# Two attentions on one core: the second attention's V in 4096 B rows, its quads in pairs, PV on 64x64 tiles, one PSUM pool

## The chip, the cores and the metric

The kernel runs on one core of one Trainium2 chip. The metric is the device time of one execution in microseconds, the median of several. A core has TensorE (PE, matmuls), VectorE (DVE), ScalarE (ACT), GpSimd (POOL) and SyncE (SP, which issues the DMAs here), each with an instruction stream of its own; semaphores order them. The matmuls' results land in PSUM, which has eight banks of 2 KB on each of 128 partitions. Transfers run on 16 DMA engines.

## The reference

Two attention blocks run on their own inputs, and their outputs are put side by side. Both have 16 batches of 32 queries, a model width of 1024, 32 query heads of 128, and a cache of 1024 keys, all in bf16. Block A has 4 key/value heads (each serves 8 query heads); block B has 32.

```python
q = (x @ wq).reshape(B, Sq, H, Dh).transpose(0, 2, 1, 3)
scores = jnp.einsum("bhqd,bhkd->bhqk", q, k_cache) * (Dh ** -0.5)
p = softmax(scores, axis=-1)
o = jnp.einsum("bhqk,bhkd->bhqd", p, v_cache)
out = o.transpose(0, 2, 1, 3).reshape(B, Sq, H * Dh) @ wo
# A: the same, with k and v repeated 8 times over the heads; result: concatenate([a, b], axis=-1)
```

The caches of B are 134 MB each for K and V, those of A an eighth of that. All that is read from memory comes to 338 MB.

## The kernel before, in words

**Quads.** The work is cut into 128 quads of A and 128 of B. A quad has 128 score rows, one for each partition. In A it is one batch and four query heads that share one K and V. In B it is two batches (`t_`) and two heads (`hh`) with 32 queries each, so four K and four V of 256 KB each belong to it. Four B quads make a group (4 batches, 4 heads, 128 tokens): the index `bp` picks the pair of batches, `hp` the pair of heads.

**A quad's chain of steps** is: scores into two PSUM banks (PE); the row maximum (DVE, `st_max`); the exponential with the row sum (ACT, `st_exp`); the transposes of P by 128 columns (PE, `st_ptr`), and their copy to `PT_sb` (`st_pev`); PV (PE, `st_pv`); the reciprocal of the sum and the normalisation (`st_norm`); the transpose of the output (`st_otr`) and its copy to `OTA_sb` or `OTB_sb`. After each group the output projection (`oproj`) adds into `acc` in SBUF. Between the quads lie the query projections of later blocks.

**Scores of B.** K of two heads of a batch is loaded in rows of 16 keys (4096 B to a partition), and DVE transposes it as 32x32 blocks of f32 into `KBt_sb` (`st_ktrB`, L785). The contraction over 128 then runs in four passes of 32x32 tiles on PE (L827): a pass of a quad has eight matmuls on eight of the 16 tiles, two row tiles to each bank. The queries are brought to the same form by `qprepB_tr` and `qprepB_sh` (`Qshuf`, L638).

**PV of B.** V is loaded by `vsrc` (L763) as eight keys of one head to a partition, 2048 B at a time. Two adjacent bf16 probabilities are transposed as one f32 by four 128x128 transposes (L862). PV has four column tiles of 32, one for each batch and head, and eight steps over the keys (L892):

```python
last = e.matmul(bank(vb)[32 * a:32 * a + 32, 0:Dh], ptc_of(vPT, c, 32 * a, 32 * a + 32), VB_sb[:, kvs, a // 2, a % 2, c, :],
                start=(c == 0), stop=(c == NCH - 1), tile_position=(0, 32 * a))
```

**Buffers.** K of B has two sides of two slots of 512 KB (`KB_sb`), with two more sides for the transposed K. V of B has three sides of two (`VB_sb`). The scores have two fixed pairs of banks (`ps_s`); a pool of four banks (`ps_g`) serves all else.

**What sets the order.** The steps are recorded in a `Prog`, and `list_schedule` lays them out in time: it takes prices for every step from `DUR` and for every packet from `PACKET`, keeps a time at which each engine is free, and picks by priority (the length of the chain behind a step, less `STEP_US` for each quad number). Buffers of a pool (`Virt`) get their place then. For steps marked "any" it chooses ACT or DVE. The result is a fixed order for every engine; at run time only semaphores decide. All loads are issued by SP in that order, so a load that waits for its buffer holds back the loads behind it.

Of the kernel before, what the change touches and what calls it, by code (L numbers as in the profile page):

```python
# [16 lines left out]
NVB_SLOTS = 3  # L17
NKB_SLOTS = 2
# [7 lines left out]
PRIO_BONUS = {}  # L26
PE_MODE = {"scoresB": 2, "Qshuf": 2, "PVB": 1}
MODE_SWITCH = 0.05
LOOK = 0.35
STEP_US = 3  # L30
STEP_NEAR = 0
ACT_FIRST = 0.3
# [3 lines left out]
    "scoresB": (0.216, 0.20), "scoresA": (0.216, 0.20), "PT_trA": (0.49, 0.22), "PT_trB": (0.49, 0.22), "PVA": (0.45, 0.22), "PVB": (0.112, 0.22),  # L36
    "OT_tr": (0.056, 0.22), "KTA_tr": (0.45, 0.22), "Qshuf": (0.107, 0.20), "qprojA": (0.432, 0.20), "qprojB": (0.432, 0.20),
    "oprojA": (0.432, 0.20), "oprojB": (0.432, 0.20), "xT_tr": (0.45, 0.22),
    "exp": (1.10, 0.12), "PT_ev@act": (0.466, 0.13), "norm@act": (0.25, 0.13), "OT_ev@act": (0.11, 0.13), "KTA_ev@act": (0.466, 0.13),
# [8 lines left out]
PACKET = {"kb_dma": (4096, 0.159), "wq_dma": (1024, 0.046)}  # L48
PACKET_DEFAULT = (2048, 0.084)
# [5 lines left out]
def dma_time(op):  # L55
    size, us = PACKET.get(op.name, PACKET_DEFAULT)
    return op.dur / size * us / 16


class _Op:  # L60
    __slots__ = ("eng", "emit", "deps", "sig", "dma_key", "dma_val", "clock", "name", "needs_sig", "waits", "dur", "t0", "t1", "tag", "prio", "idx", "alts", "step")
# [28 lines left out]
SLOTS = {"bank": 4, "P": 3, "PT": 3, "stat": 6, "O": 2}  # L90
BANK_RESERVE = {"pj": 2}


def actual(res):
    out = []
    for r in res:
        if not isinstance(r, Virt):
            out.append(r)
        elif r.cls == "bank":
            out.append(("bank", 4 + r.idx))  # L100
        else:
            out.append((r.cls, r.idx))
    return tuple(out)


class Prog:
# [12 lines left out]
    def add(self, eng, emit, reads=(), writes=(), dma_key=None, name="", dur=None, tag=None, prio=0, wtag=None, rtag=None, claims=()):  # L119
# [7 lines left out]
        if dma_key is None:  # L127
            dur = DUR.get(name, (0.2, 0.1))
        self.specs.append((eng, emit, tuple(reads), tuple(writes), dma_key, name, dur, tag, prio))
# [6 lines left out]
        op.step = self.step  # L136
        op.idx = len(self.ops)
        deps = {}
# [22 lines left out]
        if dma_key is not None:  # L161
            op.dma_key = dma_key
            self.dma_count[dma_key] = self.dma_count.get(dma_key, 0) + 1
# [59 lines left out]
    def list_schedule(self, lat=0.05, look=LOOK):  # L223
        ops = self.ops
        n = len(ops)
        users = [[] for _ in range(n)]
        ndeps = [0] * n
        for op in ops:
            ndeps[op.idx] = len(op.deps)
            for d in op.deps:  # L230
                users[d.idx].append(op.idx)

        def odur(op):
            if op.dma_key is not None:
                return DMA_FIRST + dma_time(op) + DMA_LAST
            return op.dur[0] + op.dur[1]
        bl = [0.0] * n
# [28 lines left out]

        def slot_time(i):

            t = 0.0
            for v in acq[i]:  # L270
                idle = [slot_free[v.cls][x] for x in range(SLOTS[v.cls]) if held[v.cls][x] is None]
                keep = sum(k for kind, k in BANK_RESERVE.items() if kind != v.kind and not any(h is not None and h.kind == kind for h in held["bank"])) if v.cls == "bank" else 0
                if len(idle) <= keep:
                    return None
                t = max(t, sorted(idle)[0])
            return t

        def acquire(i, st):
            for v in acq[i]:
                x = min((x for x in range(SLOTS[v.cls]) if held[v.cls][x] is None), key=lambda x: slot_free[v.cls][x])  # L280
                held[v.cls][x] = v
                v.idx = x

        def release(i, t):
            for v in mentions[i]:
                left[v] -= 1
                slot_free[v.cls][v.idx] = max(slot_free[v.cls][v.idx], t)
                if left[v] == 0:
                    held[v.cls][v.idx] = None
# [12 lines left out]
        dma_free = [0.0]  # L302

# [7 lines left out]
        while True:  # L311
            best = None
            bkey = None
            for eng, lst in ready.items():
# [11 lines left out]
                for i in lst:  # L326
                    s_ = slot_time(i) if acq[i] else 0.0
                    if s_ is not None:
                        at[i] = max(ready_t[i], fe, s_) + sw(i)
                if not at:  # L330
# [21 lines left out]
            if beng == "pe":  # L352
                pe_mode[0] = PE_MODE.get(op.name, 0)
            op.t0 = st
# [10 lines left out]
            order.append(best)  # L365
# [759 lines left out]
```

## Time and profile before

| | us |
|---|---|
| median of 3 runs | 903.28 |
| lowest and highest | 902.01, 904.05 |
| the profiled execution, own time | 904.35 |
| its span, first to last instruction | 902.6 |
| busy: PE, DVE, ACT | 836.3, 745.3, 610.8 |

The profile is of one execution. Its own time is 1.75 us above its span, and 1.07 us above the median of the runs. PE's busy time holds matmuls whose ends are modelled and which overlap, so a busy PE is not one at its peak; PEld is the loading of weights, beside it. SPq is the sequencer that issues the DMAs; its waits are for buffers. The granted clock of PE is 0.985 over the span. The page's groups give these durations, as the mean of one instruction: DVE's transpose of K (L785) 1231 ns, the maximum (L837) 1209, the exponential (L850) 1119, the normalisation on ACT (L908) 370.

### The profile page before, as it was taken

To read this page: it belongs to the slowest core of one execution; us is meant where nothing else is said; L and a number is where in the kernel's file an instruction comes from. 1 tells how busy PE (TensorE), PEld (TensorE's weight loads), DVE (VectorE), ACT (ScalarE), POOL (GpSimd) and SP (SyncE) were. 2 spreads that over 40 slices of the span, in tenths; PEclk is the share of its full clock that TensorE was granted. 3 is DMA by queue.
4 is the path that set the end of the run, shared out by engine and by line. 5 is a ranking of instruction groups with operands and counts; after the bars stand their busy time and mean duration, and the time that the engine had idled before them with its cause. 6 is when DMAs were issued, how large, how long until landed. Compare 5 with 4: busy or idle time off the path is not lost.

```text
span 902.6 us, 29455 instructions
## 1 busy us (share of the span) xinstructions
PE 836.3 (93%) x12864; PEld 481.8 (53%) x12864; DVE 745.3 (83%) x1057; ACT 610.8 (68%) x1384; POOL 1.1 (0%) x8
## 2 busy tenths in 40 slices
PE   6999999999899999999999998999998988999886
PEld 4365555555555555555545455555555554555453
DVE  0578897888887999689887899878979788798885
ACT  3477886677666776676776466776867666586763
POOL 0000000000000000000000000000000000000000
PEclk9999999999999999999999999999999999999999
DMA  9999999999999999999999999999999999999994
GB/s 325 383 389 393 386 385 392 390 393 383 392 387 389 393 380 388 380 386 376 387 385 391 394 369 389 388 393 370 388 387 391 392 391 367 344 393 393 393 377 170
DMA packets 153984, 341.67 MB, mean 379 GB/s; under 512 B 12544, under 2 KB 28928, under 8 KB 153856
## 3 DMA queue, kind: packets, MB, share of 16 engines
q1 hardware_dynamic: 153856, 339.79, 100.6%
q8 instruction: 102, 1.67, 0.8%
q14 instruction: 26, 0.21, 0.1%
HBM read 337.64 MB, written 2.10 MB: 376 GB/s over the span
## 4 chain that ended last, share of the span: by engine, by line
PE 48%; DMA 23%; DVE 19%; ACT 8%; SPq 1%; issue 1%; ACTq 0%; DVEq 0%
DMA KB_sb<-in_B_k_cache_dram 21%; PE ps_s L827 10%; PE ps_g L862 9%; DVE stat L837 8%; DVE KBt_sb L785 8%; PE ps_g L680 6%; ACT P_sb L850 5%; PE ps_g L892 4%; PE ps_g L598 4%; PE ps_g L884 4%; PE ps_g L616 3%; PE ps_s L806 3%; PE ps_g L776 2%; ACT PT_sb L526 1%; PE ps_g L914 1%
## 5 line engine op out<-in xcount | busy, mean ns | idle before, releaser
L785 DVE STREAM_TRANSPOSE KBt_sb<-KB_sb 128x1024 f32<-128x1024 f32 x256 | 311.8, 1231 | 42.5 <-DMA KB_sb<-in_B_k_cache_dram 40.4
L837 DVE TENSOR_REDUCE stat<-ps_s 128x1 f32<-128x1024 f32 x256 | 304.7, 1209 | 50.7 <-PE ps_s L827 34.3
L850 ACT ACTIVATE P_sb<-ps_s,stat 128x1024 bf16<-128x1024 f32 x256 | 285.8, 1119 | 51.5 <-DVE stat L837 50.0
L862 PE MATMUL ps_g<-id,P_sb 128*128 128x128 f32 x1024 | 177.0, 300 | 13.0 <-ACT P_sb L850 4.7
L862 PEld LDWEIGHTS ps_g<-id,P_sb 128*128 128x128 f32 x1024 | 150.5, 207 | 54.9 <-issue 11.1
L827 PE MATMUL ps_s<-KBt_sb,QR 32*32 32x512 bf16 x4096 | 157.2, 399 | 19.5 <-ACT P_sb L850 10.9
L526 ACT COPY PT_sb<-ps_g 128x512 f32<-128x512 f32 x234 | 134.9, 591 | 59.5 <-PE ps_g L862 58.3
L908 ACT ACTIVATE O_sb<-ps_g,stat 128x128 bf16<-128x128 f32 x199 | 71.4, 370 | 63.0 <-PE ps_g L892 32.4
L806 PE MATMUL ps_s<-KTA_sb,QT_sb 128*128 128x512 bf16 x256 | 91.5, 388 | 6.0 <-ACT P_sb L850 5.6
L827 PEld LDWEIGHTS ps_s<-KBt_sb,QR 32*32 32x32 bf16 x4096 | 49.3, 90 | 81.1 <-ACT P_sb L850 17.8
L892 PE MATMUL ps_g<-VB_sb,PT_sb 128*32 128x128 bf16 x4096 | 91.1, 224 | 1.4 <-ACT PT_sb L526 0.9
L892 PEld LDWEIGHTS ps_g<-VB_sb,PT_sb 128*32 128x32 bf16 x4096 | 60.2, 97 | 48.7 <-issue 29.2
L884 PE MATMUL ps_g<-VA_sb,PT_sb 128*128 128x128 bf16 x1024 | 78.8, 220 | 1.8 <-ACT PT_sb L526 0.7
L884 PEld LDWEIGHTS ps_g<-VA_sb,PT_sb 128*128 128x128 bf16 x1024 | 61.6, 98 | 28.2 <-issue 8.5
L616 PE MATMUL ps_g<-wq_sb,xT_sb 128*128 128x512 bf16 x256 | 71.4, 386 | 2.9 <-DMA wq_sb<-in_B_wq_dram 2.8
L680 PE MATMUL ps_g<-woB_sb,OTB_sb 128*128 128x512 bf16 x256 | 68.7, 381 | 4.4 <-ACT OTB_sb L526 1.8
L598 PE MATMUL ps_g<-xT_sb,wq_sb 128*128 128x512 bf16 x256 | 72.0, 385 | 0.3
L680 PE MATMUL ps_g<-woA_sb,OTA_sb 128*128 128x512 bf16 x256 | 63.0, 380 | 1.3 <-DVE OTA_sb L526 1.0
L914 PE MATMUL ps_g<-ident,O_sb 128*128 128x128 bf16 x256 | 51.8, 224 | 3.0 <-ACT O_sb L908 2.0
L850 ACT ACTIVATION_READ_ACCUMULATOR P_sb<-ps_s,stat 128x1 f32 x256 | 51.8, 202 | 0.0
L526 ACT COPY OTA_sb<-ps_g 128x64 f32<-128x64 f32 x114 | 24.7, 216 | 36.7 <-PE ps_g L914 36.1
L691 DVE TENSOR_TENSOR acc<-acc,ps_g 128x512 f32<-128x512 f32 x64 | 41.2, 675 | 8.1 <-PE ps_g L680 7.6
(41 smaller groups left out, 537.5 us busy)
## 6 DMA issues: line engine op xcount, KB each, us to landing
VB_sb<-in_B_v_cache_dram SPq DMA_DIRECT2D x256, 512.0 KB, 8.1
KB_sb<-in_B_k_cache_dram SPq DMA_DIRECT2D x256, 512.0 KB, 9.2
KA_sb<-in_A_k_cache_dram SPq DMA_DIRECT2D x64, 256.0 KB, 7.7
VA_sb<-in_A_v_cache_dram SPq DMA_DIRECT2D x64, 256.0 KB, 8.1
wq_sb<-in_B_wq_dram SPq DMA_DIRECT2D x32, 256.0 KB, 8.6
wq_sb<-in_A_wq_dram SPq DMA_DIRECT2D x32, 256.0 KB, 8.8
woB_sb<-in_B_wo_dram SPq DMA_DIRECT2D x32, 256.0 KB, 9.2
woA_sb<-in_A_wo_dram SPq DMA_DIRECT2D x32, 256.0 KB, 9.1
```

Of the source, the lines that this page charges most:

```text
L526: return e.copy(dst, src) if hasattr(e, "activation") else e.tensor_copy(dst, src)
L598: last = e.matmul(bank(v)[:, 0:tn], wq_sb[:, 0, j, hc * Dh:(hc + 1) * Dh], xT_sb[:, 0, j, t0:t0 + tn], start=(j == 0), stop=(j == DJ - 1))
L616: last = e.matmul(bank(v)[:, 0:CW], xT_sb[:, 1, j, G * P:(G + 1) * P], wq_sb[:, 1, j, :], start=(j == 0), stop=(j == DJ - 1))
L680: last = e.matmul(bank(v)[:, 0:OUTW], OT[:, gp, hh, :], wo_[:, hh, oh * OUTW:(oh + 1) * OUTW], start=(hh == 0), stop=(hh == nh - 1))
L785: pr.add("dve", lambda e: e.transpose(KBt_sb[:, sl, t_, :].bitcast(F32), KB_sb[:, rs, :].bitcast(F32)), reads=[("KB", rs)], writes=[("KBt" ...
L806: pr.add("pe", lambda e, u=u: e.matmul(ps_s[:, vS.idx, u, :], qt[:, q.b, q.hh0:q.hh0 + 4, :].rearrange("p a q -> p (a q)"), KTA_sb[:, sl, ...
L827: last = e.matmul(ps_s[32 * cg:32 * cg + 32, vS.idx, g2, :].rearrange("p (s j) -> p s j", s=16), lhsT, rhs, start=(fp == 0), stop=(fp == 3 ...
L837: pr.add("dve", lambda e: e.tensor_reduce(stat[:, vst.idx, 0:1], ps_s[:, vS.idx, :, :], AXIS.XY, ALU.max, negate=True), writes=vS.res + [v ...
L850: return e.activation(dst, src, ACTF.Exp, bias=stat[:, vst.idx, 0:1], scale=1.0, accum_out=stat[:, vst.idx, 1:2])
L862: last = e.transpose(bank(vb)[:, m * P:(m + 1) * P], p32[:, m:Sk // 2:NPK], id32[:])
L884: last = e.matmul(bank(vb)[:, 0:Dh], ptc_of(vPT, c, 0, P), VA_sb[:, kvs, c, :], start=(c == 0), stop=(c == NCH - 1))
L892: last = e.matmul(bank(vb)[32 * a:32 * a + 32, 0:Dh], ptc_of(vPT, c, 32 * a, 32 * a + 32), VB_sb[:, kvs, a // 2, a % 2, c, :], start=(c == ...
```

## The change

Seven things change together.

- **V of B** is loaded like K: 16 keys of one head to a partition, 4096 B each, two heads in the partitions' halves (`st_dmaB`). A load is 512 KB as before.
- **Two quads of B go together** (`pairB_all`): the two that share batches and differ in `hp`. Their scores are recorded as one step of 16 matmuls on all 16 tiles for each pass (`st_scoresBB`); the second quad has its heads in the other half of the score rows. There are 64 pairs.
- **P of B** is transposed in 32 blocks of 64x64 in bf16, two row halves (`e_ptB`), where four f32 transposes were.
- **PV of B** runs on 64x64 tiles: a tile contracts over the 64 partitions of one head and has 256 columns, the V of both batches (`st_pvBB`). Of the result a row uses the columns of its own batch: the normalisation covers 256 columns, two transposes follow (`st_otr`), and `st_oev` copies the blocks that are wanted. The heads change places in OTB, and `oproj` picks the rows of wo to match.
- **PSUM** is one pool of eight banks. Scores take two neighbours, at one of three places.
- **Slots of K, transposed K and V of B** (4, 4 and 7) and of Qtok (4) come from pools too, each slot of V being freed by itself.
- **The planner** has other prices (among them 0.1 for a change of PE's tile shape where 0.05 stood), a term for PE's instruction supply, order constraints (`after`) and other priorities.

The core of the diff:

```diff
-SLOTS = {"bank": 4, "P": 3, "PT": 3, "stat": 6, "O": 2}
+SLOTS = {"bank": 8, "P": 3, "PT": 4, "stat": 6, "O": 3, "Qtok": 4, "kb": 4, "KBt": 4, "vb": 7}
...
-PE_MODE = {"scoresB": 2, "Qshuf": 2, "PVB": 1}
-MODE_SWITCH = 0.05
+PE_MODE = {"scoresB": 2, "Qshuf": 2, "PVB": 1, "PT_trB": 1}
+MODE_SWITCH = 0.1
...
-STEP_US = 3
+STEP_US = 6.6
...
-PACKET = {"kb_dma": (4096, 0.159), "wq_dma": (1024, 0.046)}
-PACKET_DEFAULT = (2048, 0.084)
+PACKET = {"kb_dma": (4096, 0.164), "vb_dma": (4096, 0.164), "wq_dma": (1024, 0.0475)}
+PACKET_DEFAULT = (2048, 0.0865)
+DMA_EACH = 0.0095
...
+PE_BLOCK = 128
+PE_FETCH = 5.0
...
+        def starved(i, st):
+
+            k = PE_MM.get(ops[i].name, 2)
+            if ops[i].eng != "pe" or supply[0] + k < PE_BLOCK:
+                return 0.0
+            return max(0.0, supply[1] + PE_FETCH - st - (PE_BLOCK - supply[0]) / k * ops[i].dur[0])
...
-                for t_ in range(2):
-                    vsrc = pb["v"][q.b0 + t_, q.h0:q.h0 + 2].rearrange("hh (p c) d -> p hh c d", c=NCH)
-                    pr.add("sp", lambda e, t_=t_, vsrc=vsrc: e.dma_start(VB_sb[:, sl, t_, :, :, :], vsrc), writes=[("VB", sl, t_)],
-                           dma_key=f"vb{sl}_{t_}", name="vb_dma", dur=2 * Sk * Dh * 2, wtag={("VB", sl, t_): q.kid})
+                return e.dma_start(VB_sb[:, v.idx, :, :].rearrange("p s d -> p (s d)"), src.rearrange("hh (p s) d -> (hh p) (s d)", s=16))
+            prev_dma[kind] = pr.add("sp", emit, dma_key=v, name=kind + "_dma", dur=2 * Sk * Dh * 2, after=[prev_dma[kind]] if kind in prev_dma else [], step=step)
...
+        def st_scoresBB(qs):
...
+                for t_ in range(2):
+                    for hh in range(2):
+                        for g2 in range(2):
+                            for q in qs:
+                                rg = 2 * hh + g2
+                                cg = 2 * (hh ^ q.hp) + t_
+                                lhsT = QR[32 * rg:32 * rg + 32, gp, 2 * bp + t_, q.hp, o0:o0 + 63:2]
+                                rhs = KBt_sb[32 * rg:32 * rg + 32, q.vKt[t_].idx, :].rearrange("p (s x) -> p s x", s=16)[:, :, o0:o0 + 63:2]
+                                last = e.matmul(halves(q)[32 * cg:32 * cg + 32, g2, :].rearrange("p (s j) -> p s j", s=16), lhsT, rhs,
+                                                start=(fp == 0), stop=(fp == 3), tile_position=(32 * rg, 32 * cg))
...
+            def e_ptB(e):
+                last = None
+                for s_ in range(16):
+                    for hh in range(2):
+                        x = 64 * (hh ^ q.hp)
+                        last = e.transpose(bankb(vb)[64 * hh:64 * hh + 64, s_ * 64:s_ * 64 + 64], P_sb[x:x + 64, vP.idx, s_ * 64:s_ * 64 + 64],
+                                           ident[x:x + 64, x:x + 64], tile_position=(x, 64 * hh))
+                return last
...
+        def st_pvBB(qs):
...
+                for s_ in range(s0, s0 + 4):
+                    for hh in range(2):
+                        for q in qs:
+                            c = 64 * (hh ^ q.hp)
+                            lo, hi = sorted(v.idx for v in q.vV)
+                            last = e.matmul(bank(q.vbo)[c:c + 64, 0:2 * Dh].rearrange("p (t d) -> p t d", t=2),
+                                            PT_sb[64 * hh:64 * hh + 64, q.vPT.idx, :, :].rearrange("p c q -> p (c q)")[:, s_ * 64:s_ * 64 + 64],
+                                            VB_sb[64 * hh:64 * hh + 64, lo:hi + 1:hi - lo, s_, :],
+                                            start=(s_ == 0), stop=(s_ == 15), tile_position=(64 * hh, c))
...
+        def pairB_all(qs):
+            for q in qs:
+                for t_ in range(2):
+                    st_ktrB(q, t_)
+            loadB("kb", qs[1].t + 5)
+            loadB("vb", qs[1].t + 5)
+            st_scoresBB(qs)
+            for q in qs:
+                st_max(q)
+                st_exp(q)
+            for q in qs:
+                st_ptr(q)
+                st_pev(q)
+            st_pvBB(qs)
+            for q in qs:
+                st_recip(q)
+                st_norm(q)
+                st_otr(q)
```

## The prediction

> **What bounds the kernel now.** I read the page from the top: engine shares, the slices over time, the DMA queues, then the chain that ended last.
>
> ```profile
> span 902.6 us, 29455 instructions
> ...
> PE 836.3 (93%) x12864; PEld 481.8 (53%) x12864; DVE 745.3 (83%) x1057; ACT 610.8 (68%) x1384; POOL 1.1 (0%) x8
> ...
> DMA  9999999999999999999999999999999999999994
> GB/s 325 383 389 393 386 385 392 390 393 383 392 387 389 393 380 388 380 386 376 387 385 391 394 369 389 388 393 370 388 387 391 392 391 367 344 393 393 393 377 170
> ...
> q1 hardware_dynamic: 153856, 339.79, 100.6%
> q8 instruction: 102, 1.67, 0.8%
> ```
>
> The DMA row holds a 9 in every slice but the last, and the data queue's packets fill 100.6% of the span of 16 engines: there is no slice in which a transfer could have run earlier. PE at 93% looks nearly as full, but its row counts latency tails and changes of tile shape. What tells the two apart is who waits for whom (first the engines' waits, then the DMA queue's own):
>
> ```profile
> DVE KBt_sb L785 <- DMA KB_sb<-in_B_k_cache_dram: 40.4, 39, 8.6
> ...
> PE ps_s L827 <- ACT P_sb L850: 10.9, 15, 1.8
> ```
> ```profile
> SPq L763 <- PE ps_g L892: 136.7, 69, 7.4
> SPq L750 <- DVE KBt_sb L785: 115.2, 77, 5.2
> ```
>
> The columns are the total in us, the number of waits and the longest. DVE waits for K to arrive, up to 8.6 us at once, and the scores can't start before it; PE's own largest wait is 10.9 us in all. SP, which issues every load, often waits for a slot, yet the DMA row stays at 9 meanwhile: the queue holds several loads, the page giving 8 to 9 us from issue to landing for 512 KB. So the stream of loads sets the pace, with PE and DVE close behind.
>
> Next, DMA in two 3 us windows of that full stream, one almost all 2 KB packets (695 to 698), one almost all 4 KB (404.5 to 407.5):
>
> ```profile
> DMA packets 604, 1.16 MB, mean 386 GB/s; under 512 B 38, under 2 KB 38, under 8 KB 604
> ```
> ```profile
> DMA packets 340, 1.22 MB, mean 408 GB/s; under 512 B 37, under 2 KB 37, under 8 KB 340
> ```
>
> Leaving out the packets under 512 B, these are 2.05 KB and 4.03 KB each. Further windows agree: 388 (696 to 699) at 2 KB; 414, 412 and 408 (from 628.5, 734.5 and 138) at 4 KB.
>
> Last, a stretch of PE's timeline, for the cost of tiles:
>
> ```profile
> 140.91 0.62 PE L776 MATMUL ps_g<-ident,KA_sb 128*128 128x128 bf16 x8
> 141.36 0.38 PE L806 MATMUL ps_s<-KTA_sb,QT_sb 128*128 128x512 bf16 x1
> ...
> 141.94 0.41 PE L892 MATMUL ps_g<-VB_sb,PT_sb 128*32 128x128 bf16 x16
> 142.28 0.75 PE L862 MATMUL ps_g<-id,P_sb 128*128 128x128 f32 x4
> 142.87 0.59 PE L680 MATMUL ps_g<-woB_sb,OTB_sb 128*128 128x512 bf16 x2
> 143.39 1.13 PE L827 MATMUL ps_s<-KBt_sb,QR 32*32 32x512 bf16 x32
> 144.46 0.61 PE L680 MATMUL ps_g<-woB_sb,OTB_sb 128*128 128x512 bf16 x2
> ```
>
> From start to start, eight full transposes took 0.45 us, 56 ns each, with no gap behind them. Sixteen PV matmuls on 32-column tiles took 0.34: four waves of four at 56 ns are 0.22, so about 0.1 us went to the change of shape. Two matmuls of 512 columns took 0.44 (144.46 to the row after it, at 144.90), but 0.52 ahead of the scores (142.87 to 143.39): 0.1 again. The 32 score matmuls took 1.07, four waves of eight.
>
> **Part 1: V in rows of 4096 B, on the path.** V of the second attention is 256 loads of 512 KB, 134.2 MB, today in 2 KB packets. At the mean of the 2 KB windows (387 GB/s) it takes 346.8 us, at that of the 4 KB windows (410.5) 327.0: 19.8 us less. The planner's own packet prices in the code (0.084 and 0.159 us) give 65,536 x 0.084/16 - 32,768 x 0.159/16 = 18.4. Ends: 386 against 414 gives 23.5, 388 against 408 gives 17.0. I take 19. As nothing hides the stream, all of it counts, as long as the stream stays full.
>
> The Trainium skill, DMA: Bandwidth & Descriptors (Specifications), puts the minimum transfer for line rate at 512 B; by that both forms are at line rate and this part brings nothing. The windows above disagree, 386 against 408 GB/s.
>
> **Part 2: PE's work**, by rows and the built program's order; it lies beside the stream, so the sum only has to stay under it.
> - Scores: 4096 matmuls as before, but two quads fill 16 tiles where 8 were used. Before: 1.07 us a quad, 137 in all. If the second eight overlap, a pair costs some 1.2, 77 in all: -60. If they don't, 0.
> - PV: a wave goes from 128 to 256 columns. Before 0.56 us a quad (a run of 32 from 864.57 to 865.13), 72. After, 16 waves a pair at 0.11 (two 56 ns) plus a change, 1.86: 119, +47. If the two row halves don't run together: 32 waves, 3.6 a pair, +160.
> - P transposes of this attention: four f32 ones take 0.59 with their change, 0.48 without. After, 32 of 64x64: two side by side at 28 ns (half of 56) are 0.45 a quad, about 0; at 56 a wave +53; one after another at 56 +170. I take 0: a shape half as wide is nearest to half the time.
> - Output transposes: 128 more at 56 ns, +7.
> - Changes of tile shape: counted in the two orders, 790 become 668, at 0.1 us: -12.
>
> Sum -18, bounds -18 to about +330. I keep PE where it is, in the low 90s per cent of the span. Joint scores have direct evidence: today's waves of eight already let two row tiles write one bank on different partitions.
>
> PE's instructions grow from 12,864 matmuls to 16,576, each with its load. q8 fetches them: 102 packets, 0.8% of the span or 7.2 us of all engines; 29% more is 2.1 us, on the path.
>
> **Part 3: DVE, ACT, SP.** Most copies and normalisations of these outputs go to ACT. DVE loses 35 normalisations (about 12 us), 22 OTB copies (4.7) and 9 KTA copies (6) and gains a few: near 725 of 745. ACT gains about 18, to 630. A 128x256 normalisation should cost about the 381 ns of the 128x256 QR copy, against 370 for 128x128. Neither engine becomes the bound. The changed access pattern of exp is taken at the present 1119 ns; 10% either way, on 128 of them, is 14 us of ACT, which has over 250 idle. SP issues as many V loads; each now waits for one slot of seven instead of one side of three, and whatever stands behind a waiting V load, K too, waits with it. The reserve of 8 to 9 us covers that: zero, and if the cover goes it is rival 2.
>
> Sum: -19 + 2.1 = about -17. The profiled execution took 904.35 us (1.75 over its span), 1.07 above the median of 903.28. From the median: **886 us**. Head and tail stay: the last V is issued at 885 us, and the work behind it (PV, normalisation, output projection, store) keeps its steps.
>
> **Rivals.**
> 1. *The gain is partly given back*, 891 to 903. Four K tiles are freed together by a joint scores step, four V slots by a joint PV, so slots come free in bursts, and the stream may thin between them. For: slices of 344 to 370 GB/s already exist. 17 us over 64 pairs is 0.27 us a pair, so 0.15 us lost per pair leaves 896.
> 2. *Slower: the K loop through the transposed buffers.* All four KBt slots stay taken until the pair's last score matmul; only then can the next four transposes begin (4 x 1.23), and the scores wait for them. DVE's whole work is 725/64 = 11.3 us a pair; with it idle through the scores (1.2) and two handovers the loop is near 12.9, against a period of (886 - 30)/64 = 13.4, with 30 us set aside for head and tail (a slice of the page is 22.6). It holds by half a microsecond. If the scores stand behind other PE work or for four free banks by 1 us more than that, the loop is 14.4, and the time 30 + 64 x 14.4 = 952; it decides from 0.27 us a pair beyond the margin. Against it: DVE can do maxima during the scores, and the extra V slot adds reserve.
> 3. *PV or transposes run one tile after another*: PE near 836 + 160 busy, time about 1000. The Trainium skill, TensorEngine Tiling (Array Packing) (Gotcha 1: PSUM Pressure), says different row tiles cannot use one PSUM bank at the same time, and the new PV writes a quad's bank from both row halves; the trace's waves of eight speak against.
> 4. *Packet size does nothing*, and the lower rate of the 2 KB windows is a matter of place or time: 903.3 plus 2.1 for instruction fetches, 905. Against: six windows, in different parts of the span, order themselves by packet size. The line-rate rule of the Trainium skill, named above, would give this outcome.
>
> **Chances.** Forecast 0.62 (own range 878 to 891: V's ends, and 5 us either way in how full the stream stays); rival 1 0.19; rival 2 0.11; rival 3 0.04; rival 4 0.04. A difference under 0.2%, about 1.8 us, can hardly be told from none here. Rival 1 may give everything back (0.02 of its 0.19), and 905 is at the edge of what can be told, so half of rival 4 counts as the same: same 0.04. Faster is the forecast and the rest of rival 1, 0.79; slower is rivals 2 and 3 and the other half of rival 4, 0.17. The range reaches from 875 (23.5 saved and 5 us of thin slices closed) to 903, all of rival 1; rivals 2, 3 and 4 (0.19) stay outside.
>
> **What would show it.** Right: V's packets at 4 KB (about 121,000 packets in all), the DMA row still at 9 and GB/s above 393 in many slices, PE near 820 busy. Wrong in part 1: 4 KB packets, but GB/s no higher. Rival 2: DVE waiting for PE or SP for the KBt transposes, and slices of DMA below 9. Rival 3: PV near 230 us on PE. Any slice row with holes between the pairs would break the forecast.

## The result, and the profile after

The changed kernel takes 915.6 us (median of 4 runs, 915.07 to 916.3); the kernel before, on the same chip, 903.66. The ratio is 1.0133, with a 95% interval from 1.0113 to 1.0153: 1.3% slower, where 886 us and 2% faster had been forecast. The profiled execution took 915.24 us, 1.84 above its span. The page after:

```profile
span 913.4 us, 36884 instructions
...
PE 845.4 (93%) x16576; PEld 531.0 (58%) x16576; DVE 725.3 (79%) x996; ACT 640.3 (70%) x1445; POOL 1.1 (0%) x8
...
DMA  9999999999999999999999999999999999999992
GB/s 330 383 395 404 403 386 393 389 352 387 351 360 394 405 382 391 388 395 356 394 387 379 402 361 399 395 392 389 382 396 388 401 404 375 370 361 363 366 362 74
DMA packets 121245, 342.15 MB, mean 375 GB/s; under 512 B 12544, under 2 KB 28928, under 8 KB 121088
...
q1 hardware_dynamic: 121088, 339.79, 98.2%
q8 instruction: 131, 2.15, 0.9%
...
PE 68%; ACT 17%; DVE 9%; issue 3%; DMA 2%; SPq 1%; ACTq 0%; DVEq 0%
```

The packets came out as described (121,245), and the DMA row still shows a 9 nearly everywhere. Some slices reach 405 GB/s, more than any slice before (394), but others lie near 350 to 366. The last line is the chain that ended last, by engine. The same line of the kernel before:

```profile
PE 48%; DMA 23%; DVE 19%; ACT 8%; SPq 1%; issue 1%; ACTq 0%; DVEq 0%
```

DMA's share of the chain fell from 23% to 2%, and PE's rose from 48% to 68%. "issue" is time in which an engine waits for nothing that the profile shows; it rose from 1% to 3%. In the waits after (total us, times, longest), the K loads no longer hold DVE up:

```profile
DVE stat L911 <- PE ps_g L899: 73.3, 49, 4.1
...
PEld ps_g L983 <- issue: 14.6, 23, 2.2
...
DVE KBt_sb L854 <- DMA KB_sb<-in_B_k_cache_dram: 13.7, 3, 10.6
```

The wait of the K transposes for DMA was 40.4 us in 39 waits, and is 13.7 in 3. DVE now waits for scores instead. A stretch of PE's timeline after shows what PE waits for:

```profile
395.21 0.94 PE L899 MATMUL ps_g<-KBt_sb,QR 32*32 32x512 bf16 x46 [1.23 <-issue]
...
400.04 0.53 PE L937 MATMUL ps_g<-ident,P_sb 64*64 64x64 bf16 x22
401.41 0.34 PE L937 MATMUL ps_g<-ident,P_sb 64*64 64x64 bf16 x10 [0.84 <-issue]
...
405.51 1.94 PE L983 MATMUL ps_g<-VB_sb,PT_sb 64*64 64x256 bf16 x64
407.38 0.75 PE L948 MATMUL ps_g<-id,P_sb 128*128 128x128 f32 x4
...
409.34 1.19 PE L899 MATMUL ps_g<-KBt_sb,QR 32*32 32x512 bf16 x64
```

The run of 32 transposes (L937) breaks off after 22 and goes on 0.84 us later, in the middle of one step whose data are all there. At 395.21 the last 46 of a pair's 64 score matmuls begin, after a gap of 1.23 us of the same kind. Such gaps of the matmuls add up to 18.0 us in the waits after (22 gaps, longest 1.9) and to none in those before; 5.6 of them lie at L983, 3.4 at L899, 3.3 at L937. The sizes of the new steps are as forecast: PV of a pair 1.87 us from its start to the next (405.51 to 407.38), the joint scores 1.13 (the row after theirs starts at 410.47).

### The profile page after: what moved, and what is told of

Its sections match the earlier page's. It is cut to its first block, busy times and chain, and to the rows that moved or that the text cites. A ratio compares the mean times of both kernels' runs of the same rounds, so it can differ in the third digit from the quotient of the medians.

```text
span 913.4 us, 36884 instructions
## 1 busy us (share of the span) xinstructions
PE 845.4 (93%) x16576; PEld 531.0 (58%) x16576; DVE 725.3 (79%) x996; ACT 640.3 (70%) x1445; POOL 1.1 (0%) x8
## 2 busy tenths in 40 slices
DMA packets 121245, 342.15 MB, mean 375 GB/s; under 512 B 12544, under 2 KB 28928, under 8 KB 121088
## 3 DMA queue, kind: packets, MB, share of 16 engines
q8 instruction: 131, 2.15, 0.9%
## 4 chain that ended last, share of the span: by engine, by line
PE 68%; ACT 17%; DVE 9%; issue 3%; DMA 2%; SPq 1%; ACTq 0%; DVEq 0%
PE ps_g L983 12%; PE ps_g L748 10%; ACT P_sb L924 9%; PE ps_g L899 7%; PE ps_g L948 7%; PE ps_g L937 7%; DVE stat L911 6%; PE ps_g L968 5%; PE ps_g L660 5%; ACT O_sb L1002 4%; PE ps_g L875 4%; PE ps_g L684 4%; PE ps_g L844 2%; DVE KBt_sb L854 2%; PE ps_g L1011 2%
## 5 line engine op out<-in xcount | busy, mean ns | idle before, releaser
L911 DVE TENSOR_REDUCE stat<-ps_g 128x1 f32<-128x1024 f32 x256 | 303.8, 1215 | 102.6 <-PE ps_g L899 73.3
L924 ACT ACTIVATE P_sb<-ps_g,stat 128x1024 bf16<-128x1024 f32 x256 | 285.7, 1119 | 41.9 <-DVE stat L911 40.4
L854 DVE STREAM_TRANSPOSE KBt_sb<-KB_sb 128x1024 f32<-128x1024 f32 x256 | 302.4, 1217 | 13.8 <-DMA KB_sb<-in_B_k_cache_dram 13.7
L1002 ACT ACTIVATE O_sb<-ps_g,stat 128x256 bf16<-128x256 f32 (+1 forms) x234 | 90.8, 419 | 94.7 <-PE ps_g L968 45.1
L983 PE MATMUL ps_g<-VB_sb,PT_sb 64*64 64x256 bf16 x4096 | 131.0, 274 | 7.2 <-issue 5.6
L983 PEld LDWEIGHTS ps_g<-VB_sb,PT_sb 64*64 64x64 bf16 x4096 | 107.8, 108 | 28.7 <-issue 14.6
L937 PEld LDWEIGHTS ps_g<-ident,P_sb 64*64 64x64 bf16 x4096 | 74.5, 111 | 52.6 <-ACT P_sb L924 35.2
L937 PE MATMUL ps_g<-ident,P_sb 64*64 64x64 bf16 x4096 | 87.4, 195 | 18.7 <-ACT P_sb L924 13.9
L948 PE MATMUL ps_g<-id,P_sb 128*128 128x128 f32 x512 | 92.1, 302 | 4.4 <-ACT P_sb L924 3.5
L948 PEld LDWEIGHTS ps_g<-id,P_sb 128*128 128x128 f32 x512 | 73.6, 208 | 28.4 <-ACT P_sb L924 19.5
L875 PE MATMUL ps_g<-KTA_sb,QT_sb 128*128 128x512 bf16 x256 | 86.3, 386 | 2.1 <-issue 1.5
L899 PE MATMUL ps_g<-KBt_sb,QR 32*32 32x512 bf16 x4096 | 79.9, 394 | 4.7 <-issue 3.4
L899 PEld LDWEIGHTS ps_g<-KBt_sb,QR 32*32 32x32 bf16 x4096 | 46.0, 89 | 32.7 <-issue 12.7
```

Of the source, the lines that this page charges most:

```text
L854: op = pr.add("dve", lambda e: e.transpose(KBt_sb[:, vKt.idx, :].bitcast(F32), KB_sb[:, vK.idx, :].bitcast(F32)), reads=[vK], writes=[vKt] ...
L875: op = pr.add("pe", lambda e, u=u: e.matmul(halves(q)[:, u, :], qt[:, q.b, q.hh0:q.hh0 + 4, :].rearrange("p a q -> p (a q)"), KTA_sb[:, sl ...
L899: last = e.matmul(halves(q)[32 * cg:32 * cg + 32, g2, :].rearrange("p (s j) -> p s j", s=16), lhsT, rhs, start=(fp == 0), stop=(fp == 3), ...
L911: pr.add("dve", lambda e: e.tensor_reduce(stat[:, vst.idx, 0:1], halves(q), AXIS.XY, ALU.max, negate=True), writes=[q.vS, vst], name="max")
L924: return e.activation(dst, src, ACTF.Exp, bias=stat[:, vst.idx, 0:1], scale=1.0, accum_out=stat[:, vst.idx, 1:2])
L937: last = e.transpose(bankb(vb)[64 * hh:64 * hh + 64, s_ * 64:s_ * 64 + 64], P_sb[x:x + 64, vP.idx, s_ * 64:s_ * 64 + 64], ident[x:x + 64, ...
```

## The experiments

Comparisons are with the kernel before on the same chip, whose median lay between 902.6 and 904.1. Kernels that keep their order of steps are compared with the kernel that they come from; what a new order alone does is measured at the end.

### How much the packets are worth

V in 4096 B rows, alone, in the kernel before (V's rows then hold other keys than the probabilities that meet them):

```diff
-vsrc = pb["v"][q.b0 + t_, q.h0:q.h0 + 2].rearrange("hh (p c) d -> p hh c d", c=NCH)
-e.dma_start(VB_sb[:, sl, t_, :, :, :], vsrc)
+vsrc = pb["v"][q.b0 + t_, q.h0:q.h0 + 2].rearrange("hh (p s) d -> (hh p) (s d)", s=16)
+e.dma_start(VB_sb[:, sl, t_, :, :, :].rearrange("p hh c d -> p (hh c d)"), vsrc)
```

> The kernel before with V of the second attention loaded in 4096 B rows (16 keys of one head to a partition) and nothing else changed, in the same order of instructions; PV then pairs the probabilities with other keys, so the output is not the reference's. Stream theory (the loads set the pace of the kernel before, as the prediction had it): about 885, 903.7 less the 18 to 19 us of V packets. Compute theory (PE's work in its fixed order sets nearly the same pace, and the full DMA row only shows that loads run ahead): 898 to 904.

Measured 893.28 us (891.63 to 894.33), ratio 0.9881 [0.9856, 0.9905]: 10 us, about half of the 19. And the other way round, V of the kernel after in 2048 B packets, its order kept:

```diff
-e.dma_start(VB_sb[:, v.idx, :, :].rearrange("p s d -> p (s d)"), src.rearrange("hh (p s) d -> (hh p) (s d)", s=16))
+e.dma_start(VB_sb[:, v.idx, :, :].rearrange("p (hh c) d -> p hh c d", hh=2), src.rearrange("hh (p c) d -> p hh c d", c=8))
```

> The changed kernel with V of the second attention loaded in 2048 B packets as before (same slots, same order); PV then pairs the probabilities with other keys. If the changed kernel still gains the 18 us of packets and loses some 30 elsewhere: about 934. If its compute sets the pace and the stream has slack: 915 to 922.

Measured 918.61 (916.68 to 920.73), ratio 1.0168 [1.0141, 1.0194]: there the packets are worth some 3 us, hardly more than none (the interval overlaps that of the kernel after). The stream itself took less time with 4096 B packets in both orders. By the shares of q1 its packets took 908 us in the kernel before (100.6% of 902.6) and 888 with V in 4096 B rows (99.5% of 892.5); here they took 914 (99.9% of 914.8), and 897 in the kernel after. So the rest of the change costs 915.6 - 893.3 = 22 us at equal packets.

To see what is left when the stream is not the limit, half of V's bytes were left out of the loads after the first eight quads, in the kernel before (one head of two) and in the kernel after (half of each row, so its packets are of 2048 B):

```diff
+hn = 2 if q.t < 8 else 1
-e.dma_start(VB_sb[:, sl, t_, :, :, :], vsrc)
+e.dma_start(VB_sb[:, sl, t_, 0:hn, :, :], vsrc[:, 0:hn])
...
-e.dma_start(VB_sb[:, v.idx, :, :].rearrange("p s d -> p (s d)"), src.rearrange("hh (p s) d -> (hh p) (s d)", s=16))
+sn = 16 if q.t < 8 else 8
+e.dma_start(VB_sb[:, v.idx, 0:sn, :].rearrange("p s d -> p (s d)"), src.rearrange("hh (p s) d -> (hh p) (s d)", s=16)[:, 0:sn * Dh])
```

> The kernel before with half of each V load of the second attention left out after the first eight quads (67 MB less, about 170 us of stream), same order; it shows what the rest of the kernel needs. Stream theory: 860 or less, PE's 782 us of work and its waits. Compute theory: 890 to 900.

> The changed kernel with half of each V load of the second attention left out after the first eight quads, same order. If its stream thins for lack of free slots (the loads still set the pace, in bursts): 880 or less. If PE's order and waits set the pace: 905 to 914.

Before: 892.08 (889.16 to 895.13), ratio 0.9874 [0.9843, 0.9905]. After: 903.21 (901.1 to 907.82, 10 runs), ratio 1.0002 [0.9983, 1.0021]. The page of the first, span and chain:

```profile
span 890.6 us, 29455 instructions
...
PE 67%; DVE 19%; ACT 11%; DMA 2%; issue 1%; SPq 1%; ACTq 0%; DVEq 0%
```

With some 63 MB less to load (half of 134.2 MB, 120 of 128 quads), the kernel before is only 11 us faster, and the chain is PE and DVE. The engines' own work had a floor 11 us under the stream, so the 4096 B rows could bring no more than that: they brought 10. The floor of the kernel after is 11 us higher.

### Which part of the rest costs 22 us

Pairs with joint scores and the pools, but V in 2048 B packets and the transposes of P and PV as before (12,864 matmuls; a new order):

```diff
-PE_MODE = {"scoresB": 2, "Qshuf": 2, "PVB": 1, "PT_trB": 1}
+PE_MODE = {"scoresB": 2, "Qshuf": 2, "PVB": 1}
...
-pr.add("pe", e_ptB, reads=[vP, "ident", vPT], writes=[vb], name="PT_trB")
+pr.add("pe", e_pt, reads=[vP, "id32", vPT], writes=[vb], name="PT_trB" if q.pi else "PT_trA")
...
+last = e.matmul(bank(q.vbo)[32 * r:32 * r + 32, 0:Dh], ptc_of(q.vPT, c, 32 * r, 32 * r + 32), VB_sb[:, q.vV[t_].idx, 8 * hh + c, :],
+                start=(c == 0), stop=(c == NCH - 1), tile_position=(0, 32 * r))
```

> The changed kernel with V's packets, the P transposes, PV, normalisation and output transposes of the kernel before; what stays of the change is the joint scores, the pools and the planner. If PE's work sets the floor that the half-V runs showed (892 before, 903 after): PE is rid of the wider PV, so the floor falls by some 50 us or more, the stream of 2 KB packets is the only bound left, and the time is 885 to 897. If the pairs themselves (slots that come free in bursts, a joint step that waits for four K) cost the time: 905 to 920.

Measured 900.22 (898.52 to 902.58, 10 runs), ratio 0.9969 [0.9952, 0.9986]. That lies between the two expectations. Of the kernels here in which every product is the reference's, it is the fastest, 0.3% under the kernel before and 1.7% under the kernel after. PE is busy for 775.1 us, 61 less than before, and the time hardly falls. Its waits say why:

```profile
PEld ps_g L945 <- ACT P_sb L924: 110.9, 176, 2.9
DVE stat L911 <- PE ps_g L899: 81.6, 59, 4.2
```

PE waits for the exponentials, those for the maxima on DVE, and those for the scores: the three engines pace each other. The granted clock is also lower in this run, 0.971 against 0.985 before; taken on 775 us of PE that is up to 11 us, an estimate that no run here tests. With V in 4096 B rows in the same order (the keys then don't match):

> The kernel of pairs alone with V loaded in 4096 B rows, same order; PV then pairs the probabilities with other keys. With PE below the stream, the packets should now be worth what the windows said: 16 to 20 us less than pairs alone, 868 to 880. If compute still sets the pace: within 5 us of pairs alone.

Measured 899.3 (898.51 to 900.5), ratio 0.9952 [0.9937, 0.9966]: the packets are worth 1 us, which can't be told from nothing.

Next the instructions of PV. Eight 64x32 tiles of 128 columns in place of four 64x64 tiles of 256 (20,544 matmuls instead of 16,576; a new order):

```diff
-c = 64 * (hh ^ q.hp)
...
-                VB_sb[64 * hh:64 * hh + 64, lo:hi + 1:hi - lo, s_, :],
...
+for t_ in range(2):
+    c = 64 * (hh ^ q.hp) + 32 * t_
+    last = e.matmul(bank(q.vbo)[c:c + 32, 0:Dh],
+                    PT_sb[64 * hh:64 * hh + 64, q.vPT.idx, :, :].rearrange("p c q -> p (c q)")[:, s_ * 64 + 32 * t_:s_ * 64 + 32 * t_ + 32],
+                    VB_sb[64 * hh:64 * hh + 64, q.vV[t_].idx, s_, :],
```

> The changed kernel with PV on eight tiles of 64x32, 128 columns each (one batch to a tile), in place of four of 64x64 with 256 columns of which a row uses half; normalisation and output transposes are then as wide as before. PE work theory: PV falls from 131 to about 70 us, and the time from 915.6 to 875 to 890. Rival, PE's instruction supply: 20,544 matmuls with their loads in place of 16,576, 160 fetches; if supply is what made the waits, no better than 905.

Measured 1032.7 (1018.59 to 1040.77), ratio 1.1375 [1.1292, 1.1457], with PE busy for only 829.4 us in its profiled execution. That one is the longest of the four (1040.77 us), at a granted clock of 0.93, and the other three have 0.938 to 0.949 where the kernel after has 0.983 to 0.990: taken on PE's busy time, the clock can be up to some 46 us of what was lost, an estimate. Its waits:

```profile
PEld ps_g L983 <- issue: 85.6, 70, 4.5
PE ps_g L983 <- issue: 65.2, 38, 4.4
```

The largest waits of PE are for no engine and no transfer; "issue" makes 13% of the chain. That gave a new theory: PE runs out of instructions. PV on 128 columns in the order after, the number of instructions unchanged (half of each product is left out), was the first test of it:

```diff
-last = e.matmul(bank(q.vbo)[c:c + 64, 0:2 * Dh].rearrange("p (t d) -> p t d", t=2),
+last = e.matmul(bank(q.vbo)[c:c + 64, 0:Dh],
...
-                VB_sb[64 * hh:64 * hh + 64, lo:hi + 1:hi - lo, s_, :],
+                VB_sb[64 * hh:64 * hh + 64, lo if s_ % 2 else hi, s_, :],
```

> The changed kernel, same order of steps, with PV's matmuls on 128 columns in place of 256 (V of one batch alone is used, so half of the sum is left out). It takes some 55 us of PE's work away and no instruction. If PE's work sets the floor: 880 to 890, where the stream ends it. If the waits from step to step set it, as pairs alone suggest (68 us less work, 3 us less time): 905 to 914.

Measured 911.41 (905.37 to 914.88, 7 runs), ratio 1.0088 [1.006, 1.0115]. 1024 waves of 56 ns instead of 110 are 55 us less for PE, and the time falls by 4 in the medians. In the two profiled executions, both at a granted clock of 0.985, it is 10 (905.4 against 915.2); the other six runs here have 0.970 to 0.979. Two things take the place of PE's work: in the chain "issue" has 6% instead of 3%, and DVE 25% instead of 9%. The matmuls' gaps of 0.3 us and more that are put down to "issue" grow from 16.9 to 39.5 us: shorter matmuls reach the end of the supply sooner.

Then the transposes of P, in the order after and with four f32 ones of 128x128 in place of 32 (the probabilities then don't lie where PV expects them; 12,992 matmuls, 483 changes of tile shape in place of 668):

```diff
-for s_ in range(16):
-    for hh in range(2):
-        x = 64 * (hh ^ q.hp)
-        last = e.transpose(bankb(vb)[64 * hh:64 * hh + 64, s_ * 64:s_ * 64 + 64], P_sb[x:x + 64, vP.idx, s_ * 64:s_ * 64 + 64],
-                           ident[x:x + 64, x:x + 64], tile_position=(x, 64 * hh))
+p32 = P_sb[:, vP.idx, :].bitcast(F32)
+for m in range(NPK):
+    last = e.transpose(bank(vb)[:, m * P:(m + 1) * P], p32[:, m:Sk // 2:NPK], id32[:])
```

> The changed kernel, same order of steps, with the second attention's P transposes made of four 128x128 f32 transposes as before in place of 32 of 64x64 in bf16 (the probabilities then don't stand where PV expects them). It takes away 3584 of PE's 16,576 matmuls with their loads, 185 changes of tile shape, and little work. If PE's instruction supply and the changes of shape make PE's extra waits: 895 or less. If the pairs' waits do: 908 to 916.

Measured 891.67 (891.59 to 893.67), ratio 0.988 [0.9864, 0.9896]: 24 us back. It changes both the number of instructions and the shape changes. So the shape was kept in the next one, with four matmuls of 512 columns on the same 64x64 tiles:

```diff
+for u in range(2):
+    for hh in range(2):
+        x = 64 * (hh ^ q.hp)
+        last = e.matmul(bank(vb)[64 * hh:64 * hh + 64, 0:512], ident[x:x + 64, x:x + 64], P_sb[x:x + 64, vP.idx, u * 512:u * 512 + 512], start=True, stop=True, tile_position=(x, 64 * hh))
```

> The kernel after in its own order, but the 32 transposes of B's probabilities become four matmuls on the same 64x64 tiles with 512 columns each (identity as weights; the probabilities are copied and not transposed, so what PV multiplies is not the transposed matrix). 3584 matmuls and loads fewer (12,992), the 668 changes of tile shape stay, and the PE time of the step stays near 0.5 us. Theory 'instruction supply' (fewer matmul-and-load pairs remove the stalls): 890 to 898, as with the four f32 transposes. Rival 'changes of tile shape' (what the four f32 transposes removed were 185 changes at 0.1 us): 910 to 916, no gain. In between: both have a part.

Measured 893.38 (891.33 to 895.52), ratio 0.9898 [0.9868, 0.9928]: 22 us, with all 668 shape changes. Its page:

```profile
PE 831.9 (93%) x12992; PEld 471.7 (53%) x12992; DVE 724.2 (81%) x996; ACT 639.2 (72%) x1445; POOL 1.1 (0%) x8
...
q8 instruction: 103, 1.69, 0.8%
...
PE 58%; ACT 20%; DVE 15%; DMA 4%; issue 2%; SPq 1%; ACTq 0%; DVEq 0%
```

The fetches fall from 131 packets to 103, and the matmuls' "issue" gaps from 18.0 us to 4.3. The wide matmuls stream the probabilities, where the transposes load them as weights; that is not where the gain lies, as PE waits as long for them at this step (14.1 us, 13.9 in the kernel after), and the four f32 transposes load them too. The step is also a little shorter, 552 ns against 624 from its start to the next (medians). A counterpart, with the shape changes taken away and the instructions kept (31 matmuls of 8 columns and one of 512), was meant to complete the pair:

> The kernel after in its own order, but the 32 transposes of B's probabilities become 31 matmuls of 8 columns and one of 512 on the full 128x128 tile (what PV multiplies is not the transposed matrix). The number of matmuls and loads stays at 16,576, the changes of tile shape fall to the 483 that the four f32 transposes gave. Theory 'instruction supply': 912 to 925, no gain. Rival 'changes of tile shape': 890 to 900. If 31 short matmuls take much longer than 0.3 us together, PE gets more work and the run is read by that: its group row decides whether it can be used.

Measured 972.23 (962.84 to 973.92), ratio 1.0746 [1.0691, 1.0801]. It can't be used for its question: the short matmuls ran on 128x32 tiles and took 0.87 us, the step 1.19 instead of 0.62, 73 us more of PE over 128 quads. It shows only that PE's time is on the path: 57 of the 73 us came through. That is why the shorter step had to be separated too, by a padding of 160 columns that makes it as long as the 32 transposes (13,248 matmuls):

```diff
-for u in range(2):
+for lo, hi in ((0, 512), (512, 1024), (0, 160)):
```

> The kernel after in its own order with the 64x64 copies of 512 columns as in the run before (probabilities copied, not transposed), and two more matmuls of 160 columns, so that the step takes PE as long as the 32 transposes did (552 ns in the run with four wide matmuls, 624 in the kernel after: 0.07 us, 128 times, 9 us). 13,248 matmuls instead of 16,576, shape changes as after. Theory 'instruction supply': 893 to 899, so at least 16 of the 22 us stay gained at the same PE time. Rival 'PE time of the step': what the wide matmuls gained was PE's 9 us and what hangs on it, 902 or more.

Measured 899.35 (894.91 to 900.19, 7 runs), ratio 0.9945 [0.9924, 0.9965]: at the edge of what the supply predicted. At about the same PE time, 16 of the 22 us stay gained; the other 6 go with the 9 us of PE's time.

Last, the same replacement in the order of the kernel before, with V in 4096 B rows (893.28 us): the change's 32 transposes there, and the four wide matmuls as the control.

> The kernel before with V in 4096 B rows (893.3 us) in its own order, and B's four f32 transposes replaced by the change's 32 bf16 transposes on 64x64 tiles (V's keys and the probabilities don't meet in this form). 3584 matmuls and loads more, two more shape changes for most of the 128 quads. Theory 'instruction supply': as much more than the next run (four wide matmuls on the same tiles) as the change itself loses, 13 to 22 us above it: 908 to 925. Rival 'shape changes or PE time': at most 9 us above the next run.

> The same as the run before this one, but with four matmuls of 512 columns on the 64x64 tiles in place of the 32 transposes: the shape changes alone, no more instructions. Theory 'instruction supply': 893 to 900. Rival 'shape changes': up to 256 more at 0.1 us, 26 us: up to 915.

The 32 transposes: 936.39 (935.73 to 939.05), ratio 1.0368 [1.0342, 1.0394]. The control, with the same tiles: 896.94 (895.45 to 900.79), ratio 0.9932 [0.9906, 0.9957]. The control has 177 more changes of shape than the kernel before (967, counted in the traces' order) and is some 4 us longer than it with the same rows of V. The 3584 additional matmuls with their loads cost 39, of which up to 9 could be the length of the step (624 ns and 552 here too); the supply theory had expected 13 to 22. The page of the first, and its waits:

```profile
PE 852.1 (91%) x16448; PEld 484.6 (52%) x16448; DVE 741.8 (79%) x1057; ACT 611.4 (65%) x1384; POOL 1.1 (0%) x8
...
q8 instruction: 130, 2.13, 0.9%
...
PE 73%; DVE 12%; ACT 9%; issue 4%; DMA 1%; SPq 1%; ACTq 0%; DVEq 0%
```
```profile
PEld ps_g L904 <- issue: 40.0, 82, 2.6
...
PEld ps_g L863 <- issue: 26.4, 59, 1.6
PEld ps_s L827 <- issue: 24.3, 47, 2.5
```

And the control's page and waits:

```profile
PE 835.3 (93%) x12864; PEld 425.4 (48%) x12864; DVE 741.4 (83%) x1057; ACT 610.9 (68%) x1384; POOL 1.1 (0%) x8
...
q8 instruction: 102, 1.67, 0.8%
...
PE 65%; DVE 18%; ACT 9%; DMA 6%; issue 1%; SPq 1%; ACTq 0%; DVEq 0%
```
```profile
PEld ps_g L904 <- issue: 31.4, 77, 0.5
PEld ps_g L863 <- issue: 20.6, 50, 0.8
PEld ps_s L827 <- issue: 17.1, 49, 0.4
```

The totals are not far apart; the longest waits are. In the control none of the three exceeds 0.8 us: short pauses of the weight loads beside running matmuls. With 130 fetches they reach 2.6 us, and the matmuls themselves stand for 26.5 us in 31 gaps, where the control has none.

Whether these gaps are waits for instructions can be read from the trace, which has every fetch as a packet of 16 KB on q8. The gap of 0.84 us in the stretch of the kernel after ends at 401.41. The last fetch before it is this one, in the window from 398.8 to 400:

```profile
q8 instruction: 1, 0.02, 5.4%
```

The packet begins at 398.88 and has landed at 399.91, and PE goes on 1.5 us later. All the gaps are of this kind: the 22 in the kernel after end 1.29 to 1.61 us after a fetch has landed, the 31 with the 32 transposes in the order before 1.25 to 1.60, the four with four wide matmuls 1.27 to 1.59, and with 64x32 tiles 64 of the 68 gaps of 0.3 us and more end 1.0 to 1.7 us after one. A moment picked at random lies 1.0 to 1.7 us behind a fetch with a chance of about 0.1. In the first three of these kernels it is 2.3 to 2.7 us from the start of the fetch until PE goes on; PE stands when the instructions that it still has don't last that long.

### Orders and slots

Three kernels with new orders. The planner's former priorities with everything else as after (`PRIO_BONUS = {}`, `MODE_SWITCH = 0.05`, `STEP_US = 3`, `PE_FETCH = 0.0`, `LAST_STEP = 1000`):

> The changed kernel laid out with the planner's earlier settings (no priority bonus, 0.05 for a change of tile shape, STEP_US 3, no term for instruction supply). If the time lies in the order and its waits rather than in the work: different by 10 us or more, either way. If in PE's amount of work: 910 to 922.

Measured 961.89 (959.62 to 967.23), ratio 1.0652 [1.0614, 1.0689]. Six slots of K and of its transposed form instead of four (with `acc` in bf16 to make room, and loads a quad earlier):

> The changed kernel with six slots for K and six for the transposed K in place of four and four; the room comes from partial sums of the output in bf16. The planner lays it out anew. If the K loop through four slots (rival 2 of the prediction) thins the stream: 903 or less. If not: within the planner's own scatter of the changed kernel, 908 to 922.

Measured 922.74 (919.67 to 929.4), ratio 1.0235 [1.0184, 1.0285]: no gain. And `STEP_US = 6.4` instead of 6.6, nothing else:

> The changed kernel laid out with STEP_US 6.4 in place of 6.6 and nothing else: the scatter that a new order alone brings. If the time is a property of the work and the buffers: within 4 us of 915.6. If each order has its own waits: different by 5 us or more.

Measured 925.4 (923.45 to 928.38), ratio 1.0251 [1.0226, 1.0275]: 10 us from another order alone. So the kernels with new orders (pairs alone, 64x32, slots) can't be read finer than some 10 us against others; the main findings rest on kernels that keep an order.

## Why the prediction was wrong, point by point

**"As nothing hides the stream, all of it counts": the first step that failed.** A DMA row full of nines showed that the stream never rested; it did not show that the engines would follow a faster one. Their floor lay 11 us below (892.1 with half of V left out), so at most that could be had. The row that warned of it was in the page: DMA had 23% of the chain, PE 48%. The size of the packets' saving was near what was forecast: their time fell by 20 us in the order before and by 17 in the order after, and the rate rose in places (slices up to 405 GB/s). That so much would also come off the run was never seen, as the engines' floor came first. By the line-rate rule of the Trainium skill, DMA: Bandwidth & Descriptors (Specifications), 2 KB and 4 KB would give the same time; the 10 us in the order before speak against it, and the 3 us after are small because PE is the limit there, not because the packets are alike (17 us of their time).

**"The sum only has to stay under it": the same error on PE's side.** Most of PE's terms were sized well. Changes of shape took about 0.1 us each where they could be seen, PV of a pair 1.87 us (1.86 forecast), the joint scores 1.13 with their change (1.2 forecast), and the transposes 0.62 with theirs (0.59 for the four f32 ones; 0 forecast, 4 us over 128 quads). PE's busy time is 845 where "near 820" had been named. With the measured steps, from the start of one to the next, the sum is about -3 and not -18: scores -63, PV +48, transposes +5, output transposes +7 as forecast; the -12 for fewer changes of shape was counted twice, as the prices of the steps hold them already. From -3 to the +9 of the busy row is not accounted for. DVE came out as forecast (725 us), and ACT 10 us above (640 against 630): its 115 normalisations of 128x256 took 471 ns and not 381. But PE and its chain with DVE and ACT were the bound within 11 us, so a gain of PE's was not free cover, and a loss counted.

**Instruction fetch, +2.1 us: the term that was mis-sized.** It was priced as the DMA time of 29 more packets. The 28 or so that the transposes bring cost 22 us in the order after (16 at equal PE time) and 39 in the order before (30 without the length of the step). The price is paid by PE, which stands in the middle of a step until the next instructions come, not by the data queue: the matmuls' gaps behind a fetch are 18.0 us in the kernel after and 4.3 with four wide matmuls, 14 of the 22 us. With it the sum closes: 903.3 - 10 (packets) + 22 (the transposes' instructions and the step's length) is 915, and pairs, joint scores and the new PV come out near zero together, as the kernel with four wide matmuls shows (893.4, against 893.3 for the packets alone).

**The P transposes, "about 0" with ends of 0 and +170.** They are the step that lost, but by another mechanism than the one bounded: their waves overlap as taken (0.50 us for 32), and it is their number that costs.

**Rivals.** *Part of the gain given back* (0.19) is not what happened: thin slices there are (351 to 366 GB/s), but DVE waits less for K than before, and the loss comes back with PE's instructions at the same slots and the same order. *The K loop through the transposed buffers* (0.11) named the sign, but not the cause: two more slots brought no gain (in a new order, so to within some 10 us), and with the four slots unchanged 22 us came back by the transposes alone. *PV or transposes one tile after another* (0.04): 1.87 us a pair excludes it, and with it Gotcha 1 (PSUM Pressure) of the Trainium skill, TensorEngine Tiling (Array Packing), as a limit here: a quad's bank is written from both row halves, at 117 ns a wave of four (1.87 us over 16, the change included). *Packet size does nothing* (0.04): not so, 10 us in the order before; the six windows held against it were fewer, as the two of 2 KB packets (695 to 698 and 696 to 699) overlap. No rival held the cause.

**What stays open.** That the gaps of PE's matmuls are waits for instructions is read from the fetches in the trace; the moment at which a fetch is asked for, and what fills the 1.3 to 1.6 us between its landing and the next matmul, are not in it. With half of V left out of the kernel after (data packets at 87% of the span instead of 98%) a fetch took 1.07 us on the mean, against 1.05, so nothing shows that a fuller data queue lengthens it; an empty one was not tried. The 8 us of the 22 that are not in the matmuls' gaps are the shorter step, some 9 us, as far as is known. Why the same 3584 matmuls cost 39 us in one order and 22 in the other was not tried; the planner after has a term for the supply (`starved`), and an order with it set to zero was run only together with other priorities.

## What to carry to other kernels

A resource that is busy all the time gives back only as much as the next bound allows, so measure that floor (leave out half of the suspected bytes) before counting a saving in full. When a kernel is within a per cent or two of its PE, count matmul and weight-load instructions as a cost of their own, not only their columns: many short matmuls in a row can make PE wait for its program, and it shows as "issue" gaps in the middle of a step, each ending shortly after a packet of the instruction queue has landed (some 1.5 us here). Compare variants in one fixed order of steps, since another order alone moved this kernel by 10 us and more.

## What the runs showed of the hardware that was not expected

- PE's program comes in packets of 16 KB (2.15 MB in 131 packets, about 253 of the 33,152 matmuls and loads to each). 28 more of them cost 22 us (0.8 us each) and 39 us (1.4 us each), lengths of step included. The Trainium skill, Runtime: NRT & Kernel Launch (Instruction fetch mechanics), describes blocks of 16 KiB, 256 instructions, fetched while the one before is executed, and calls the cost mostly hidden. The size agrees with the trace; that it is hidden does not, where 64 instructions (32 transposes with their loads) go by in 0.50 us: there PE stood up to 1.9 us in one gap, and up to 4.4 us with 20,544 matmuls. PE went on 2.3 to 2.7 us after the start of the fetch that it stood for, in all 22 gaps of the kernel after.
- Halving the columns of 4096 matmuls took some 55 us off PE's waves and 4 us off the time (10 at an equal granted clock).
- The small matmuls of 8 columns took 28 ns each (0.87 us for 31, changes of shape included), no less than transposes of 64 columns, of which two run side by side in 32 ns.
